# A linear-attention and mixer kernel: x tile 2 loads over GpSimd's queue, and the first query stream turns it ahead of the last weight slices

## The chip, the cores and the metric

The kernel runs on one core of a Trainium2 chip. The metric is the device time of one execution in microseconds (us). The profile shows one execution: TensorE (PE, with its weight loads as PEld), VectorE (DVE), ScalarE (ACT), GpSimd (POOL), SyncE (SP) and the DMA engines. SP, ACT and POOL each have a queue on which they issue transfers.

## The reference

Input x has 2048 tokens of width 640, all in bf16. Two branches are computed from x and mixed by a gate.

```python
g = sigmoid((x * gate_w).sum(-1, keepdims=True))
# branch A: linear attention, 32 heads of 20
q, k, v = split(x @ wqkv)                  # 640 -> 3 * 640
phi = lambda t: where(t > 0, t + 1, exp(t)) + 1e-6
pq, pk = phi(q), phi(k)
kv, z = einsum("sd,se->de", pk, v), pk.sum(over tokens)      # for each head
a = (pq @ kv) / (pq @ z + 1e-6) @ wo
# branch B: layernorm, w1, gelu, shift of tokens by quarters, w2, residual x1
#           layernorm, w3 (640 -> 1728), gelu, w4, residual
out = g * a + (1 - g) * b
```

## The kernel before

The tokens lie in 16 tiles of 128 (`NT`), the width of 640 in five slices of 128 (`KD`). A small scheduler class records every operation for its engine together with the semaphores it must wait for, and each engine then runs its own list in order. The order of the main part is chosen by a planner from modelled costs (`_Items.run`); the order of the opening, which is what matters here, is written out by hand.

The opening works like this. x tiles are loaded with tokens on the partitions (`x_tok`), and the projections need them transposed (`xT`). Tiles 0, 1 and 2 are turned by PE: `t_x(t)` transposes the five blocks of a tile against an identity `ident` (line 637 in the profile) into a bank of PSUM, and VectorE copies the bank to `xT` (line 691) in one to three pieces. Tiles 3 and later are turned by a DMA transpose on SP's queue (`x_turn`, line 281). For tile 2, `t_x` also does a small matmul of `gwr`, the gate's weights, against the identity (line 606 with the tile `xn`), which lands in the same bank; VectorE's copies of that bank come after it.

The identity is made by GpSimd (a memset of `ones_c`, then a select), in the same list in which GpSimd issues the load of the gate's weights ("gw").

The query weights `wq` come in five slices of 128 rows (wq0 to wq4), each a transfer of its own, and so do the key weights (wk0 to wk4). Transfers are issued at line 285 of the profile: x0, x1, wq2, x2, wk0, wk2, x3, wk4, x4 and then the DMA turns on SP's queue; wq0, wq1, wq3, wq4, wk1, wk3 and the last columns of wq on ACT's queue.

PE's list of the opening is: warm-up matmuls on a constant (line 904), the turn of tile 0, one more small warm-up, `q_three`, `k_two`, then one key tile, and after that a query and a key tile in turn. `q_three` is a stream (line 942): an entry (t, k) is one matmul of 512 columns that adds slice k for tile t; an entry (t, None) is the turn of tile t. Tiles 0, 1 and 2 each keep a PSUM bank until their fifth slice is in; then `phi` runs: ScalarE's exponential (line 682), VectorE's clamp (line 648) and VectorE's combining step (line 665). `k_two` is the same for the keys of tiles 0 and 1, where each entry is a pair of matmuls, of 512 and 130 columns (lines 942 and 614), in the order (0,0), (0,1), (1,0), (0,2), (1,1), (0,3), (1,2), (0,4), (1,3), (1,4).

After the opening come the gram matrix of x and the keys (lines 831 and 625), the mixer's first two products, and the large products with w3 and w4 (lines 606 and 1240).

Of the kernel before, what the change touches and what calls it, by code (L numbers as in the profile page):

```python
# [416 lines left out]
def _build(nc, A_x, A_wqkv, A_wo, B_w1, B_w2, B_w3, B_w4, gate_w, out, dbg=None, stop=None):  # L417
    sch = _Sched(nc)
# [54 lines left out]
    x_tok = pa.alloc("x_tok", [128, NT, D], BF16)  # L473
# [223 lines left out]
    x2 = A_x[0]  # L697

    def dma_in(out_ap, in_ap, key, **kw):
        return sch.dma("sp", out_ap, in_ap, key, **kw)  # L700

    def load_x(t):
        dma_in(x_tok[:, t, :], x2[128 * t:128 * (t + 1), :], "x%d" % t)

    def load_wq(k, queue):
        sch.dma(queue, wq[:, k, 0:512], A_wqkv[128 * k:128 * (k + 1), 0:512], "wq%d" % k)
# [12 lines left out]
    load_wq(1, "act")  # L719
    load_wq(2, "sp")  # L720
    load_wq(3, "act")
    load_x(2)
    load_wq(4, "act")
    load_wk(0, "sp")
    load_wk(1, "act")
# [83 lines left out]
    def phi(b, dst, after_exp=None, n=D):  # L809
        se = slot("E", 3)  # L810
        src = psf[:, 512 * b:512 * b + n]
        er = Er[:, se, 0:n]
        activation(er, src, ACTF.Exp)
        if after_exp is not None:
            after_exp()
        ts(dve, er, er, 1.0, EPS_PHI, ALU.min, ALU.add)
        return stt(dst, src, 1.0 + EPS_PHI, er, ALU.add, ALU.max)
# [108 lines left out]
    def stream(order, w, n2, done):  # L926
        bs = {}
        for t in sorted({t for t, k in order if k is not None}):
            bs[t] = pair() if n2 else bank()
            bank_hold.update((bs[t], bs[t] + 1) if n2 else (bs[t],))  # L930
        for t, k in order:
            if k is None:
                if t is None:
                    warmup(256, 0.42)
                else:
                    t_x(t)
                continue
            b = bs[t]
            l = xT[:, k, 128 * t:128 * (t + 1)]

            def fn(e, l=l, b=b, k=k):
                ins = e.matmul(ps[:, b, 0:512], l, w[:, k, 0:512], start=(k == 0), stop=(k == KD - 1))  # L942
                return ins if not n2 else mm_kept(e, ps[:, b + 1, 0:n2], l, w[:, k, 512:512 + n2], k == 0, k == KD - 1)
            pe(fn, [l, w[:, k, 0:512 + n2]], [ps[:, b, 0:512]] + ([ps[:, b + 1, 0:n2]] if n2 else []), cost=272.0 if n2 else 216.0)
            if k == KD - 1:
                bank_hold.difference_update((b, b + 1) if n2 else (b,))
                done(t, b)

    def q_three():
        order = [(0, 0), (1, None), (0, 1), (1, 0), (1, 1), (0, 2), (1, 2), (0, 3), (1, 3), (2, None), (0, 4), (1, 4),  # L950
                 (2, 0), (2, 1), (2, 2), (2, 3), (2, 4)]
        stream(order, wq, 0, lambda t, b: phi(b, pq_tok[:, t + 1, 0:512], n=512))

    def k_out(t, b):
# [10 lines left out]
    addA(("tx", 0), 0.28, lambda: t_x(0))  # L965
    addA(("warm", 1), 0.0, lambda: warmup(WARM2, 0.42))
    addA(("q", 2), 3.24, q_three)
    addA(("k", 1), 2.72, k_two)
    addA(("k", 2), 1.36, lambda: k_tile(2))
# [474 lines left out]
    order = IT.run(sch, hook)  # L1444
# [6 lines left out]
def bass_gated_mix__linear_attn_block__mixer_s_mlp__prompt_kernel(  # L1451
    nc, A_x, A_wqkv, A_wo, B_x, B_w1, B_w2, B_w3, B_w4, gate_w, out
):
    assert tuple(A_x.shape) == (1, S, D) and tuple(out.shape) == (1, S, D)
    assert tuple(A_wqkv.shape) == (D, 3 * D) and tuple(A_wo.shape) == (D, D)
    assert tuple(B_w1.shape) == (D, D) and tuple(B_w2.shape) == (D, D)
    assert tuple(B_w3.shape) == (D, F) and tuple(B_w4.shape) == (F, D) and tuple(gate_w.shape) == (D,)
    _build(nc, A_x, A_wqkv, A_wo, B_w1, B_w2, B_w3, B_w4, gate_w, out)
# [28 lines left out]
```

## Time and profile before

| | us |
|---|---|
| median of 3 runs | 259.18 (258.26 to 259.21) |
| profiled execution | 259.12 |
| its span in the profile | 257.9 |
| PE busy | 254.6 (99% of the span) |
| VectorE busy | 144.1 (56%) |
| ScalarE busy | 108.5 (42%) |
| GpSimd busy | 90.6 (35%) |

A line of the timeline gives start, duration, engine, line, operation and tiles; in square brackets is the time that the engine stood idle before it, and what released it. A list of waits has the waiting engine and line, what it waited for, the total, the number of times and the longest. A line of DMA issues ends with the median time from issue to landing. The duration of one matmul (379 ns for 512 columns) includes its way through the array; matmuls in a run start 216 ns apart.

### The profile page before, as it was taken

Reading aid. Unit: us, or ns where it says so; the run is one execution under the profiler, and the core shown is the slowest. Engines: PE = TensorE matmul, PEld = TensorE weight load, DVE = VectorE, ACT = ScalarE, POOL = GpSimd, SP = SyncE. Lnnn points to the kernel's source line nnn. Section 1 sums busy time; section 2 is a strip of 40 time slices with the busy share of each in tenths; the row PEclk is TensorE's granted clock in tenths of the full one; section 3 lists DMA queues with packets and bytes.
Section 4 is the critical chain, followed back from the end, with each engine's and each line's share of the span. In section 5 each row is a group of like instructions: output and inputs, shape, how many; then the busy total and the mean of one; then the engine's idle time right before and its main releaser. Section 6 shows DMA issues by size and latency. Waiting matters only on the chain.

```text
span 257.9 us, 3612 instructions
## 1 busy us (share of the span) xinstructions
PE 254.6 (99%) x1418; PEld 110.6 (43%) x1242; DVE 144.1 (56%) x290; ACT 108.5 (42%) x222; POOL 90.6 (35%) x146
## 2 busy tenths in 40 slices
PE   8999999999999999999999999999999999999997
PEld 4333333344454333334444444444444444444444
DVE  2697888899953995489999400689300043200033
ACT  1486676751356867665854230003520100253000
POOL 5021399967762153758907100423000011300000
DMA  6767698545843699362915520022300112200002
GB/s 209 223 170 197 145 144 223 172 86 127 108 99 78 97 335 382 85 106 51 124 40 127 127 54 20 0 82 73 51 0 0 23 20 102 102 1 3 0 20 102
DMA packets 57825, 26.48 MB, mean 103 GB/s; under 512 B 49188, under 2 KB 56397, under 8 KB 57808
## 3 DMA queue, kind: packets, MB, share of 16 engines
q1 hardware_dynamic: 54976, 21.87, 35.9%
q0 software_dynamic: 1168, 3.28, 4.9%
q10 hardware_dynamic: 1664, 1.11, 1.4%
q8 instruction: 10, 0.16, 0.3%
q14 instruction: 7, 0.06, 0.1%
HBM read 12.04 MB, written 2.62 MB: 57 GB/s over the span
## 4 chain that ended last, share of the span: by engine, by line
PE 96%; DMA 2%; SPq 0%; DVE 0%; issue 0%
PE ps L606 37%; PE ps L1240 30%; PE ps L625 14%; PE ps L831 7%; PE ps L614 4%; DMA x_tok<-in_A_x_dram 2%; PE ps L942 1%; PE ps L1286 1%; PE ps L1147 1%; SPq L285 0%; PE ps L1029 0%; PE ps L1058 0%; PE ps L637 0%; DVE x_tok L665 0%
## 5 line engine op out<-in xcount | busy, mean ns | idle before, releaser
L606 PE MATMUL ps<-xnT,w 128*128 128x512 bf16 x360 | 81.3, 379 | 0.0
L665 DVE SCALAR_TENSOR_TENSOR x_tok<-ps,stg,abx 128x512 bf16<-128x512 f32 (+2 forms) x17 | 12.2, 719 | 81.5 <-PE ps L1240 81.3
L682 ACT ACTIVATE h2T<-ps 128x512 bf16<-128x512 f32 x52 | 30.6, 598 | 59.3 <-PE ps L606 59.3
L606 PEld LDWEIGHTS ps<-xnT,w 128*128 128x128 bf16 x360 | 34.5, 98 | 41.6 <-issue 2.2
L1240 PE MATMUL ps<-w,h2T 128*128 128x512 bf16 (+2 forms) x221 | 45.4, 366 | 0.0
L648 POOL TENSOR_SCALAR xn<-x_tok,st 128x640 bf16<-128x640 bf16 x32 | 35.3, 1110 | 27.8 <-DMA xnT<-xn 27.2
L648 POOL TENSOR_SCALAR abx<-x_tok,stg 128x640 f32<-128x640 bf16 (+1 forms) x16 | 14.8, 930 | 70.0 <-DVE x_tok L665 70.0
L1240 PEld LDWEIGHTS ps<-w,h2T 128*128 128x128 bf16 x221 | 21.1, 98 | 24.1
L682 ACT ACTIVATE Er<-ps 128x512 bf16<-128x512 f32 (+1 forms) x36 | 23.0, 648 | 14.8 <-PE ps L614 10.6
L681 ACT ACTIVATE junk<-x_tok 128x640 bf16<-128x640 bf16 x32 | 23.6, 738 | 3.9 <-DVE x_tok L663 3.7
L682 ACT ACTIVATE hsT<-ps 128x512 bf16<-128x512 f32 (+1 forms) x32 | 19.0, 593 | 12.6 <-PE ps L606 12.1
L625 PE MATMUL ps<-w,hsT 128*128 128x512 bf16 x80 | 23.0, 379 | 0.0
L625 PE MATMUL ps<-wkg,xT 128*128 128x512 bf16 x70 | 20.6, 379 | 0.0
L663 DVE SCALAR_TENSOR_TENSOR x_tok<-ps,x_tok 128x640 bf16<-128x640 f32 x16 | 13.2, 822 | 10.8 <-PE ps L614 10.2
L1240 PE MATMUL ps<-M_sb,pqnT 128*128 128x512 bf16 (+2 forms) x85 | 18.6, 367 | 0.0
L831 PE MATMUL ps<-pk_tok,x_tok 128*128 128x512 bf16 x80 | 17.8, 379 | 0.0
L614 PE MATMUL ps<-wkg,xT 128*128 128x130 bf16 x80 | 17.6, 220 | 0.0
L1176 DVE TENSOR_TENSOR pq_tok<-pq_tok,dnr 128x300 bf16<-128x300 bf16 (+1 forms) x48 | 17.3, 415 | 0.6
L614 PE MATMUL ps<-w,hsT 128*128 128x128 bf16 x80 | 17.5, 219 | 0.0
L606 PE MATMUL ps<-wq,xT 128*128 128x512 bf16 x65 | 16.2, 379 | 0.0
L648 DVE TENSOR_SCALAR Er<-Er 128x512 bf16<-128x512 bf16 (+1 forms) x36 | 12.2, 340 | 6.8 <-ACT Er L682 5.9
L656 DVE TENSOR_TENSOR qprod<-qprod,pk_tok 128x640 f32<-128x640 f32 x13 | 15.1, 1165 | 0.4
(90 smaller groups left out, 252.4 us busy)
## 6 DMA issues: line engine op xcount, KB each, us to landing
w<-in_B_w_dram SPq DMA_DIRECT2D x1, 2160.0 KB, 8.1
w<-in_B_w_dram SPq DMA_DIRECT2D x1, 2080.0 KB, 13.1
out_dram<-x_tok SPq DMA_DIRECT2D x3, 640.0 KB, 3.1
w<-in_B_w_dram POOLq DMA_DIRECT2D x8, 160.0 KB, 3.4
x_tok<-in_A_x_dram SPq DMA_DIRECT2D x6, 160.0 KB, 4.1
x_tok<-in_A_x_dram SPq DMA_DIRECT2D x1, 960.0 KB, 5.5
wv<-in_A_wqkv_dram POOLq DMA_DIRECT2D x1, 800.0 KB, 5.3
x_tok<-in_A_x_dram SPq DMA_DIRECT2D x1, 640.0 KB, 5.0
```

The lines of the kernel that those rows point to most:

```text
L606: ins = e.matmul(out_ap, l, r, start=(i == 0), stop=(i == n - 1))
L614: return e.add_instruction(mybir.InstMatmult(name=nc.get_next_instruction_name(), engine=e.engine, ins=[e.lower_ap(r), ll], outs=[e.lower_ ...
L625: e.matmul(outs[0], l, r, start=st, stop=sp, skip_group_check=True)
L648: return engf(lambda e: e.tensor_scalar(out_ap, in_ap, s1, s2, op0, op1), rd, [out_ap], cost=cost)
L656: return engf(lambda e: e.tensor_tensor(out_ap, a, b_, op), [a, b_], [out_ap], cost=cost)
L663: return dve(lambda e: e.scalar_tensor_tensor(out_ap, in0, scalar, in1, op0, op1, accum_out=accum), rd, [out_ap, accum], cost=cost + 70.0)
L665: return dve(lambda e: e.scalar_tensor_tensor(out_ap, in0, scalar, in1, op0, op1), rd, [out_ap], cost=cost)
L681: return act(lambda e: e.activation(out_ap, in_ap, func, bias=bias, scale=scale, accum_out=accum), rd, wr, cost=cost)
L682: return act(lambda e: e.activation(out_ap, in_ap, func, bias=bias, scale=scale), rd, wr, cost=cost)
L831: ins = e.matmul(o, l, r, start=(t0 + q_ == 0), stop=(t0 + q_ == NT - 1))
L1176: dve(lambda e, o=o, i0=i0, i1=i1: e.tensor_tensor(o, i0, i1, ALU.mult), [i0, dnr[:, 1, sd, :]], [o], cost=cost)
L1240: ins = e.matmul(o, l, r, start=first and i == 0, stop=last and i == len(prs) - 1, skip_group_check=True)
```

## The change

x tile 2 is no longer the fourth transfer of SP's queue. It is the first transfer of GpSimd's queue, ahead of the gate's weights. In the first query stream the turn of tile 2 comes right after (1,0), and (1,1), (2,0) and (2,1) follow it; slices 2, 3 and 4 of wq then meet tiles 0, 1 and 2 one after another. The number of operations is the same on every engine; on VectorE and ScalarE their order is the same too.

```diff
     load_wq(1, "act")
     load_wq(2, "sp")
     load_wq(3, "act")
-    load_x(2)
+    sch.dma("pool", x_tok[:, 2, :], x2[256:384, :], "x2")
     load_wq(4, "act")
     load_wk(0, "sp")
     load_wk(1, "act")
...
     def q_three():
-        order = [(0, 0), (1, None), (0, 1), (1, 0), (1, 1), (0, 2), (1, 2), (0, 3), (1, 3), (2, None), (0, 4), (1, 4),
-                 (2, 0), (2, 1), (2, 2), (2, 3), (2, 4)]
+        order = [(0, 0), (1, None), (0, 1), (1, 0), (2, None), (1, 1), (2, 0), (2, 1), (0, 2), (1, 2), (2, 2),
+                 (0, 3), (1, 3), (2, 3), (0, 4), (1, 4), (2, 4)]
         stream(order, wq, 0, lambda t, b: phi(b, pq_tok[:, t + 1, 0:512], n=512))
```

## The prediction

> **What bounds the kernel now.** I read the busy table first, then the waits of TensorE (PE), then the chain of waits that ended last, and only then the first ten microseconds in detail.
>
> ```profile
> PE 254.6 (99%) x1418; PEld 110.6 (43%) x1242; DVE 144.1 (56%) x290; ACT 108.5 (42%) x222; POOL 90.6 (35%) x146
> ```
>
> PE is busy for 254.6 of 257.9 us. Asked for PE's own waits over the whole span, the trace has two:
>
> ```profile
> PE ps L904 <- PEq L1472: 0.8, 1, 0.8
> PE ps L637 <- DMA x_tok<-in_A_x_dram: 0.6, 1, 0.6
> ```
>
> The first is the start of the program. The second is the only stall on data, and it is the one that this change addresses. The chain, asked for 0 to 10 us, starts with it:
>
> ```profile
> 2.18 5.05 DMA x_tok<-in_A_x_dram
> 7.23 0.05 issue
> 7.28 0.45 PE ps L637 x5
> ...
> 7.74 1.82 PE ps L942 x8
> ```
>
> x tile 2 is issued on SP's queue at 2.18, lands at 7.23, and PE turns it at 7.28. From there PE runs without a wait to the last matmuls. So a shift of the first key matmul, now at 9.18, passes to the end one for one, and nothing else in this change can matter much. The matmul rows of the first stream say how much there is to win:
>
> ```profile
> 4.95 0.92 PE L942 MATMUL ps<-wq,xT 128*128 128x512 bf16 x3
> 5.92 0.81 PE L942 MATMUL ps<-wq,xT 128*128 128x512 bf16 x3
> 7.28 0.23 PE L637 MATMUL ps<-ident,x_tok 128*128 128x128 bf16 x1 [0.55 <-DMA x_tok<-in_A_x_dram]
> ```
>
> Matmul ends are modelled; starts in a run are 0.216 us apart. The last one before the stall starts at 6.35, so PE is really free at 6.56 and loses 0.71 us, not 0.55. Last, the DMA side, by the microsecond (busy of PE, granted clock, DMA share, GB/s):
>
> ```profile
> 2.00:3.00 1.00, 1.00 (x4) 1.00 0.97 251
> 3.00:4.00 1.00, 1.00 (x8) 1.00 0.99 333
> 4.00:5.00 1.00, 1.00 (x12) 1.00 0.96 282
> 5.00:6.00 1.00, 1.00 (x7) 1.00 0.93 281
> 6.00:7.00 1.00, 0.73 (x4) 1.00 1.05 377
> ```
>
> The 16 DMA engines are full from 2 to 9 us. Bringing one tile forward pushes others back.
>
> **The work and the floor.** From the first query matmul at 4.32 to the first key matmul at 9.18 are 4.86 us. In it lie 15 matmuls of 0.216 (3.24), ten transposes of 0.056 (0.56) and the gate's small matmul (about 0.03): 3.83 us. The first matmul and the turn of tile 1 still run partly at the slower rate (4.32 to 4.95 for what should take 0.50), so about 0.9 us is waiting and 0.1 slow rate. Were every wait to go, the gain would be 0.9 us, or 0.35%. A measurement of this kernel can tell about 0.5% (1.3 us) from no change. No case in which the change works reaches that.
>
> **x2's issue.** SP loses one issue of 0.43 us, so its later ones (wk0, wk2, x3, wk4, x4) go out 0.47 us sooner. With full DMA engines they hardly land sooner, and SP then waits 4.4 us for x3 before it turns tile 3, so this is worth nothing. GpSimd gains one issue, ahead of the gate load. The issues of its queue (size, us from issue to landing), from 1 to 1.5 us and from 38.5 to 43.1, and its timeline:
>
> ```profile
> xn<-in_gate_w_dram POOLq DMA_DIRECT2D x1, 1.2 KB, 3.4
> ...
> w<-in_B_w_dram POOLq DMA_DIRECT2D x4, 160.0 KB, 2.6
> ```
>
> ```profile
> 1.33 0.76 POOL L285 DMA_DIRECT2D xn<-in_gate_w_dram  x1 [0.83 <-DVE xn L715]
> ...
> 2.39 0.29 POOL L694 TENSOR_SCALAR_AFFINE_SELECT ident<-ones_c 128x128 bf16<-128x128 bf16 x1
> ```
>
> The other queues begin at 0.79 and x2 waits for nothing, so its issue begins near 0.8. GpSimd's issues last 0.51 to 1.01 us; it ends at 1.35 to 1.8. The gate load, which now begins at 1.33 because it waits for VectorE, moves by 0.02 to 0.5. The identity, ready at 2.68, is then ready by 3.2; PE needs it at 3.71, so this is hidden with half a microsecond to spare; past that it would cost its lateness.
>
> **When x2 lands.** Bounds: 2.6 us after issue (four loads of the same shape on GpSimd's queue, later, quieter) gives 3.4; 5.1 (x2 itself on SP now) gives 5.9. I take the gate load's 3.4, the same queue at the same place, plus 160 KB at 282 GB/s (0.57): 4.8. PE will ask for it at 5.4, so I expect no stall there. The gate load, 0.02 to 0.5 later and behind x2 on its queue, lands at 4.8 to 5.6; PE asks at 5.69.
>
> **The new order on PE.** (0,0), the turn of tile 1, (0,1) and (1,0) stand at 4.32, 4.64, 4.95 and 5.18 as now. Tile 2's turn follows at 5.40, the gate's matmul at 5.69, (1,1) at 5.72. In the present trace (2,0) starts 0.52 after the gate's matmul (7.57 to 8.09: its end, then VectorE's copy of 0.22, then the semaphore). So (2,0) starts at 6.21: a new wait of 0.27 behind (1,1), with all later matmuls queued after it. From there eleven matmuls of 0.216 (2.38) end at 8.59, where the first key matmul can start: 0.58 sooner than 9.18. That is the best case of this order.
>
> **What x2 pushes back.** x2's 160 KB now go ahead of part of x1, wq1 to wq4, at 282 GB/s 0.57 us of all engines. Bounds for x1 and wq1 (the trace has their landings at 4.34 and 4.57): none, if x2 fills gaps, as the 251 GB/s of the microsecond from 2 to 3 against 377 later allows; or the whole 0.57. The whole puts tile 1's turn at 4.95, (1,0) at 5.48 and the key matmul at 8.89. Halfway is 8.74. wq4, now at 7.5 (its issue near 2.2 plus 5.3), lands at most at 8.1. Tile 0 asks for it at 7.95 to 8.1, and the key matmul is never before wq4 plus 0.65 (three matmuls), 8.75. wk1 moves from 8.3 to at most 8.85 and is wanted 0.27 after the key start. All three agree near 8.75 to 8.8.
>
> The Trainium skill, page "DMA: Bandwidth & Descriptors", section "Issuing engines are not separate DMA queues", speaks against the change: a third issuing engine runs on the same 16 DMA engines and saves only issue time. By that rule the whole 0.57 is pushed back and the gain is 0.29; by the 2 to 3 row alone it would be 0.58. The shares of 0.93 to 1.05 side with the rule from 3 us on, so I stand between.
>
> **After the stream.** The three exponentials come close together and just before the keys. ScalarE starts at wq4 plus 0.41 as now (7.60 to 8.01), VectorE needs 0.92 per tile, so tile 1's bank is free about 2.35 after the key start. The single key tile that reuses it comes ten pairs of 0.272 (2.72) after: 0.37 to spare. Tile 3's transposed copy lands near 12.1 and its query matmul starts at 13.26, so 0.4 earlier is still covered. Memory banks, and the order on VectorE and ScalarE, are the same.
>
> **Sum.** Key start 9.18 to 8.78, gain 0.40. The profiled execution took 259.12: span 257.9 and 1.2 around it. 257.9 - 0.4 + 1.2 = 258.7. The median of the three runs is 0.06 above the profiled one: 258.8.
>
> **Rivals.**
> 1. *The wait only changes its name.* The weight slices meet three tiles each, so PE now follows wq2, wq3 and wq4, and these are what x2 delays. If wq4 lands at 8.45 rather than 8.1, the key start is 9.1 to 9.2 again: 259.1. For it: full engines, and the same bytes before the keys. Against: wq4's place in ScalarE's queue is unchanged and one tile costs 0.57 at most.
> 2. *GpSimd's queue is late* (the slower side). All of the stream now stands behind x2 and the gate load. x2 after 5.4, or the gate after 5.7, moves everything; from 0.58 beyond (x2 after 5.98) the kernel is slower than before, microsecond for microsecond. The longest landing on GpSimd's queue in the trace, 5.8, puts x2 at 6.6 and the time at 259.8; the longest of any load here, 7.2 on ScalarE's queue, puts it at 8.0 and the time at 261.2. Against: the nearest row is 3.4, and x2 is first in its queue.
> 3. *The clock comes late.* PE's matmul rate doubles at 4.64, 3.8 us after the first warm-up matmul. If x2 makes x0 late, PE pauses near 3.7. If the doubling then came one such stretch later, half of 3.8 us would be lost: 1.9, less the 0.4 gained, 260.7.
> That the change does not do what it says is excluded by the order of instructions: x2 is GpSimd's first transfer, and tile 2's turn stands after five matmuls fewer.
>
> **How the numbers follow.** Forecast 0.57 (258.5 to 259.0, with a scatter of runs of 258.26 to 259.21 before: 258.1 to 259.4). Rival 1: 0.25 (259.1). Rival 2: 0.14, about half of it past 260.5. Rival 3: 0.04, all but a little past 260.5. For eight in ten the range goes from 258.1, the forecast's best with scatter, to 259.8, the first figure of rival 2. Slower by over 0.5% is half of rival 2 and most of rival 3: 0.10. Faster by over 0.5% lies past the 0.9 us that is there, so only scatter gives it: 0.04. Within 0.5%: 0.86.
>
> **What would show it.** Right: the wait of L637 for the load of x is gone from PE's list, the turn of tile 2 starts at 5.4 to 5.7, the wait before (2,0) is near 0.3, the first key matmul starts at 8.6 to 8.9, and the span is shorter by the same amount. Rival 1: waits of L942 for the wq loads, key start near 9.2. Rival 2: L637 or the gate's matmul waits for a GpSimd load. Rival 3: transposes of 0.11 us spacing after 4.7. Wrong altogether: a key start that moves and a span that doesn't follow, which would mean a second wait behind the first that the trace of before hides.

## The result, and the profile after

The changed kernel took 260.04 us in the median of 7 runs (259.49 to 260.76), the kernel before 258.92 us beside it on the same chip (258.26 to 259.21, 7 runs). The ratio is 1.0044, with an interval of 1.0027 to 1.0061: slower by 1.1 us. The prediction was 258.8, with a range of 258.1 to 259.8. The profiled execution is the fastest of the seven (259.49, span 258.2). The changed kernel was therefore run a second time beside the experiments, and that profiled execution (260.10, span 258.8) lies at the median; the text calls it the second profile.

Of PE's own waits over the whole span, as in the first step of the prediction, the one on data:

```profile
PE ps L637 <- DMA x_tok<-in_A_x_dram: 0.6, 1, 0.6
```

The wait that the change was to remove is still there, with the same name and the same length, although PE asks 1.2 us earlier. The timeline of PE (start, duration, line, operation; in brackets the idle time before it):

```profile
4.92 0.60 PE L942 MATMUL ps<-wq,xT 128*128 128x512 bf16 x2
6.09 0.45 PE L637 MATMUL ps<-ident,x_tok 128*128 128x128 bf16 x5 [0.56 <-DMA x_tok<-in_A_x_dram]
6.66 0.18 PE L606 MATMUL ps<-ident,xn 128*128 128x5 bf16 x1
6.70 3.01 PE L942 MATMUL ps<-wq,xT 128*128 128x512 bf16 x12
9.54 0.38 PE L942 MATMUL ps<-wkg,xT 128*128 128x512 bf16 x1
```

The second matmul of the first line starts at 5.15, so PE is free at 5.37 and asks for x2 as predicted (5.4). The turn starts at 6.09, not at 5.4. Its five transposes take 0.056 each, so the gate's matmul could stand at 6.38; it stands at 6.66. The first key matmul is at 9.54, not at 8.78, and 0.36 later than in the kernel before (9.18). What holds the gate's matmul is named in the chain of waits:

```profile
1.34 0.81 POOL x_tok L285
2.15 4.46 DMA xn<-in_gate_w_dram
...
6.66 0.19 PE ps L606
...
6.87 0.24 DVE xT L691
...
7.15 2.76 PE ps L942 x12
```

The start of the chain is now GpSimd's queue. Nothing is issued on it before 1.34; then x2's issue takes 0.81, and the gate's load, 1.2 KB, is issued only at 2.15 and lands at 6.61. VectorE's copy of tile 2 needs the gate's matmul, (2,0) needs the copy, and all later matmuls of PE stand behind (2,0).

In the second profile, at the median, the same two waits are larger. PE's timeline there:

```profile
5.27 0.60 PE L942 MATMUL ps<-wq,xT 128*128 128x512 bf16 x2
6.36 0.45 PE L637 MATMUL ps<-ident,x_tok 128*128 128x128 bf16 x5 [0.49 <-DMA x_tok<-in_A_x_dram]
7.36 0.18 PE L606 MATMUL ps<-ident,xn 128*128 128x5 bf16 x1 [0.55 <-DMA xn<-in_gate_w_dram]
7.40 3.01 PE L942 MATMUL ps<-wq,xT 128*128 128x512 bf16 x12
10.25 0.38 PE L942 MATMUL ps<-wkg,xT 128*128 128x512 bf16 x1
```

Here x2 lands at 6.31 and the gate at 7.32, and the key start is 10.25: 1.07 later than before, which is the size of the whole loss.

**Everything passes to the end.** Time of the profiled execution less the start of the first key matmul: 259.12 - 9.18 = 249.94 for the kernel before, 259.49 - 9.54 = 249.95 and 260.10 - 10.25 = 249.85 for the changed one. In the profiles of all the experiments it is 249.82 to 249.95. So each kernel below can be read by one number, its key start, and that number by what lands last ahead of it.

### The profile page after: what moved, and what is told of

Its sections match the earlier page's. It is cut to its first block, busy times and chain, and to the rows that moved or that the text cites. A ratio compares the mean times of both kernels' runs of the same rounds, so it can differ in the third digit from the quotient of the medians.

```text
span 258.2 us, 3585 instructions
## 1 busy us (share of the span) xinstructions
PE 253.0 (98%) x1391; PEld 110.7 (43%) x1242; DVE 144.2 (56%) x290; ACT 108.6 (42%) x222; POOL 90.8 (35%) x147
## 4 chain that ended last, share of the span: by engine, by line
PE 90%; DVE 5%; DMA 2%; ACT 1%; issue 1%; POOL 0%; POOLq 0%
PE ps L606 34%; PE ps L1240 30%; PE ps L625 12%; PE ps L831 7%; PE ps L614 4%; PE ps L942 2%; DMA xn<-in_gate_w_dram 2%; DVE x_tok L663 1%; PE ps L1286 1%; DVE dnr L1157 1%; DVE pq_tok L1176 1%; ACT hsT L682 1%; PE ps L1147 1%; DVE qprod L656 1%; PE ps L1029 0%
## 5 line engine op out<-in xcount | busy, mean ns | idle before, releaser
L606 PE MATMUL ps<-xnT,w 128*128 128x512 bf16 x348 | 79.9, 379 | 0.6 <-issue 0.2
L682 ACT ACTIVATE hsT<-ps 128x512 bf16<-128x512 f32 (+1 forms) x32 | 19.0, 594 | 12.6 <-PE ps L606 11.1
```

The costliest lines, as they stand in the source:

```text
L606: ins = e.matmul(out_ap, l, r, start=(i == 0), stop=(i == n - 1))
L682: return act(lambda e: e.activation(out_ap, in_ap, func, bias=bias, scale=scale), rd, wr, cost=cost)
```

## The experiments

The theory after the result: the new order makes the way from x2 to the keys longer, and GpSimd's queue brings x2 and the gate too late for it. The rivals: it is the queue alone (x2 pushes the query weights back, whatever the order); it is the order alone (the queue does not matter); and, for the late landings, that GpSimd's part in the DMA traffic, or something of ScalarE's, makes them late.

The table has all kernels beside the kernel before of their own chip. "x2" and "gate" are the landings of the last part of each transfer (a transfer is spread over 16 DMA engines; PE waits for the last of the 16 parts), "key" is the start of the first key matmul, all in the profiled execution. "ACT" is ScalarE's queue, "3rd" the place on a queue.

| kernel | x2 on | gate on | order | x2 | gate | key | profiled | median | ratio (interval) |
|---|---|---|---|---|---|---|---|---|---|
| before | SP, 4th | GpSimd | old | 7.23 | 4.74 | 9.18 | 259.12 | 258.92 | 1 |
| changed | GpSimd | GpSimd, 2nd | new | 6.05 | 6.61 | 9.54 | 259.49 | 260.04 | 1.0044 (1.0027 to 1.0061) |
| changed, second time | GpSimd | GpSimd, 2nd | new | 6.31 | 7.32 | 10.25 | 260.10 | 260.04 | 1.0041 (1.0026 to 1.0056) |
| load alone | GpSimd | GpSimd, 2nd | old | 6.87 | 7.37 | 9.91 | 259.75 | 259.72 | 1.0024 (1.0007 to 1.0041) |
| order alone | SP, 4th | GpSimd | new | 6.43 | 4.72 | 9.66 | 259.49 | 260.09 | 1.0048 (1.0027 to 1.0068) |
| gate off GpSimd | GpSimd | ACT, 3rd | new | 6.00 | 4.39 | 9.35 | 259.18 | 259.21 | 1.0006 (0.9995 to 1.0017) |
| x2 on ScalarE | ACT, 3rd | GpSimd | new | 6.65 | 5.27 | 9.89 | 259.75 | 259.54 | 1.0020 (1.0001 to 1.0039) |
| nothing on GpSimd, old order | SP, 4th | ACT, 3rd | old | 6.78 | 4.50 | 9.34 | 259.17 | 259.15 | 1.0006 (0.9996 to 1.0017) |
| nothing on GpSimd, new order | ACT, 3rd | SP, 3rd | new | 6.21 | 4.50 | 9.45 | 259.27 | 259.27 | 1.0013 (1.0004 to 1.0021) |
| early exponential | SP, 4th | GpSimd, late | old | 6.90 | 10.02 | 12.81 | 262.65 | 261.91 | 1.0115 (1.0099 to 1.0131) |
| gate's matmul apart | GpSimd | GpSimd, 2nd | new | 6.97 | 7.48 | 10.20 | 260.15 | 259.41 | 1.0019 (1.0006 to 1.0031) |
| gate apart, turn later | GpSimd | GpSimd, 2nd | another | 6.12 | 6.96 | 9.43 | 259.25 | 259.26 | 1.0012 (0.9998 to 1.0025) |
| load alone, gate apart | GpSimd | GpSimd, 2nd | old | 6.06 | 6.58 | 9.16 | 258.99 | 259.37 | 1.0021 (1.0007 to 1.0034) |
| x2 third on SP | SP, 3rd | GpSimd | new | 6.41 | 4.97 | 9.87 | 259.70 | 259.48 | 1.0020 (1.0009 to 1.0030) |

A profiled execution is one draw: the same x2 transfer, fourth on SP's queue, landed at 7.23, 6.43, 6.78 and 6.90 in four kernels. Size is therefore read from the ratios, mechanism from the profiles.

### The load alone

On the kernel before, with its order:

```diff
-    load_x(2)
+    sch.dma("pool", x_tok[:, 2, :], x2[256:384, :], "x2")
```

> Only the load is moved: x2 is GpSimd's first transfer, the stream keeps its old order. Theory A (the changed kernel loses because x2 and the gate load come late over GpSimd's queue and the new order puts the whole stream behind them): x2 lands near 6.05 and the gate near 6.6 as in the changed kernel, but the old order asks for them only at 6.56, so the stall on x2 falls from 0.7 to 0.1 us, the first key matmul starts at 9.0 to 9.1 and the time is 0.1 to 0.2 us below before (258.7 to 258.8). Theory C (x2's early bytes push the weight slices back): wq4 lands at 8.0 or later, seven matmuls follow it, the first key matmul starts at 9.5 or later, 0.3 to 0.5 us above before (259.3).

The ratio is 1.0024, and the wait has another name in PE's list:

```profile
PE ps L942 <- DMA wq<-in_A_wqkv_dram: 1.2, 2, 1.1
```

This is the prediction's first rival, in a kernel other than the one it was meant for: x2 goes ahead of the query weights, and these are what PE asks for first in the old order. wq2 lands at 6.78 and wq3 at 7.54; in the kernel before they landed at 5.34 and 5.60, and PE did not wait for them. It is their last parts that come late: the middle part of wq2 landed at 4.65, sooner than the 4.90 of the kernel before, and the last 2.1 us behind it. That x2's bytes hold those last parts back is argued and not shown; with the same transfers wq2 landed at 5.88 and 4.90 in the two profiles of the changed kernel. The turn of tile 2 stands behind (1,3), so x2 at 6.87 is early enough, and the gate at 7.37 too.

### The order alone

The new `order` of `q_three`, with x2 fourth on SP's queue.

> Only the order is changed: tile 2 is turned right after (1,0), but x2 stays the fourth transfer of SP's queue. Theories A and B (the order itself costs) agree: PE stands from 5.4 until x2 lands near 7.2, (2,0) starts 0.8 us after that, eleven matmuls follow, the first key matmul starts near 10.4 to 10.5 and the time is 1.2 to 1.4 us above before (260.2). It gives the price per us of lateness of x2 in this order. Theory C: the same.

The ratio is 1.0048, as much as that of the whole change:

```profile
6.47 0.45 PE L637 MATMUL ps<-ident,x_tok 128*128 128x128 bf16 x5 [0.94 <-DMA x_tok<-in_A_x_dram]
```

From x2's landing at 6.43 to the key start are 3.23 us. With the same transfer in the old order it was 7.23 to 9.18, that is 1.95. The 1.28 between them are five more matmuls behind the turn (twelve, not seven: 5 x 0.216 = 1.08) and some 0.2 of the wait before (2,0), which (1,1) alone covers now. The same 3.23 to 3.24 stand in the kernels with x2 on ScalarE, with nothing on GpSimd in the new order and with the gate's matmul apart. So the new order needs x2 by 9.18 - 3.23 = 5.95, and no profile has it before 6.00. The 9.18 is that of one execution (259.12). The median of the kernel before, 258.92, answers to a key start of 258.92 - 249.95 = 8.97, and by that the new order needs x2 by 5.74 already.

Load alone (0.6 us) and order alone (1.2) do not add up to the change (1.1). The likely reason, not tested by itself: with the load the weights come later, but the new order asks for them later too.

### The gate's load off GpSimd's queue

On the changed kernel; the gate's load becomes the third transfer of ScalarE's queue:

```diff
     load_wq(1, "act")
+    sch.dma("act", xn[0:KD, 1, 0:128], gate_w.rearrange("(k p) -> k p", p=128), "gw")
...
-    sch.dma("pool", xn[0:KD, 1, 0:128], gate_w.rearrange("(k p) -> k p", p=128), "gw")
```

> The changed kernel, but the gate's weights load as the third transfer of ScalarE's queue, so they no longer stand behind x2 on GpSimd's. Theory A: the gate lands before 5.2, the wait of its matmul (0.27 us in the profiled execution) goes, x2 still lands near 6.05, the first key matmul starts near 9.25 and the time is about 0.3 us below the changed kernel (259.6 to 259.8). Theory B: no gain, since the order is kept (260.0). Theory C: no gain or 0.1 us.

The ratio falls from 1.0041 to 1.0006: 0.9 of the 1.1 us are gone, and the kernel can no longer be told from the kernel before.

```profile
6.04 0.45 PE L637 MATMUL ps<-ident,x_tok 128*128 128x128 bf16 x5 [0.49 <-DMA x_tok<-in_A_x_dram]
6.33 0.17 PE L606 MATMUL ps<-ident,xn 128*128 128x5 bf16 x1
```

The gate's matmul follows the last transpose at once (6.33, where the second profile of the changed kernel has 1.0 from the turn to it). The wait for x2 stays. The key start is x2 + 3.35: by x2 it would be 9.23, and the rest is wq4, which lands at 8.64 behind the gate's load on its queue. The 0.9 need not be the gate's landing alone: here GpSimd issues one load less, and x2's first data moved at 3.67, where the two profiles of the changed kernel have 4.04 and 4.16.

### x2 on ScalarE's queue

On the changed kernel; GpSimd has the gate's load alone again:

```diff
     load_wq(1, "act")
+    sch.dma("act", x_tok[:, 2, :], x2[256:384, :], "x2")
...
-    sch.dma("pool", x_tok[:, 2, :], x2[256:384, :], "x2")
```

> The changed kernel's order, with x2 as the third transfer of ScalarE's queue (ahead of wq3) instead of GpSimd's; the gate load stays GpSimd's only early transfer. Theory A: x2 lands at 5.2 to 5.6, the gate at 4.7, the order finds its data in time, the first key matmul starts at 8.6 to 8.9 and the time is 0.3 to 0.6 us below before (258.3 to 258.6). Theory B: the order costs whatever the queue, so it stays 0.5 us or more above before (259.4 or more). Theory C: wq3 and wq4 are pushed back by a whole tile, the first key matmul starts near 9.2 or later and the time is that of before or 0.3 us above (259.0 to 259.2).

```profile
6.70 0.45 PE L637 MATMUL ps<-ident,x_tok 128*128 128x128 bf16 x5 [1.02 <-DMA x_tok<-in_A_x_dram]
```

x2, issued at 1.72, lands at 6.65: 4.9 us from issue to landing, where GpSimd's queue took 4.7 and 5.0. The ratio is 1.0020 (259.54, in the range of theory B). The middle one of its 16 parts lands at 5.29, the last 1.36 us behind it. So a slow GpSimd queue is not what makes x2 late; a wait of half a microsecond to one for x2 stays whichever queue it is on.

### The changed kernel again

> The changed kernel once more, beside the kernels of this call. All theories: 259.9 to 260.3, 0.8 to 1.2 us above before. Its profiled execution was its fastest (259.49); theory A says that an execution of the median time has the gate's last part, behind x2, landing near 7.2 instead of 6.61, and the first key matmul near 10.1 instead of 9.54; were the key start not later than 9.6 in an execution near 260.0, the loss would lie elsewhere.

The result repeats: 260.04 again, 1.0041. Its timeline is shown with the result above. PE waits in it for both loads, and its landings say what each costs when the execution is a median one. The sum closes: x2 at 6.31 + 3.23 = 9.54 is 0.36 more than before; the gate adds 10.25 - 9.54 = 0.71. Together 1.07.

### Nothing on GpSimd's queue, in both orders

If GpSimd's traffic were what makes the last parts late, they should come in time without it. In the old order:

```diff
     load_wq(1, "act")
+    sch.dma("act", xn[0:KD, 1, 0:128], gate_w.rearrange("(k p) -> k p", p=128), "gw")
...
-    sch.dma("pool", xn[0:KD, 1, 0:128], gate_w.rearrange("(k p) -> k p", p=128), "gw")
```

> The kernel before, but the gate's weights load as the third transfer of ScalarE's queue: GpSimd's queue carries nothing in the opening. In every profile so far the DMA rate falls from 330 to 380 GB/s to 150 to 250 between 4 and 5.5 us, and some of the 16 DMA engines fall a microsecond behind. Theory D1 (GpSimd's first transfers make that dip): the dip is gone, x2 lands at 6.2 to 6.4 instead of 7.23, PE does not stand, the first key matmul starts at 8.5 to 8.6 and the time is 0.4 to 0.6 us below before. Theory D2 (ScalarE's table load at 4.14 makes it) and D3 (neither): the dip stays, x2 lands near 7, the time is that of before within 0.2 us.

Here x2's landing decides nothing. The gate's load stands ahead of wq3 on ScalarE's queue, wq3 lands at 6.96 (5.60 in the kernel before), and PE waits for it before it asks for x2:

```profile
PE ps L942 <- DMA wq<-in_A_wqkv_dram: 0.9, 1, 0.9
```

So this kernel answers the question on the rate, but its time says nothing of what an earlier x2 would be worth.

In the new order the gate's load is third on SP's queue and x2 third on ScalarE's:

```diff
     load_x(1)
+    sch.dma("sp", xn[0:KD, 1, 0:128], gate_w.rearrange("(k p) -> k p", p=128), "gw")
     load_wq(1, "act")
+    sch.dma("act", x_tok[:, 2, :], x2[256:384, :], "x2")
...
-    sch.dma("pool", x_tok[:, 2, :], x2[256:384, :], "x2")
...
-    sch.dma("pool", xn[0:KD, 1, 0:128], gate_w.rearrange("(k p) -> k p", p=128), "gw")
```

> The changed kernel's order with x2 as the third transfer of ScalarE's queue and the gate's weights as the third of SP's: GpSimd's queue carries nothing in the opening. D1: no dip, x2 lands by 5.5, the first key matmul starts at 8.6 to 8.9, 0.3 to 0.6 us below before (258.5). D2 and D3: x2's last part lands near 6.5 as with GpSimd's gate load (6.65), the key start is 9.6 to 9.9 and the time 0.4 to 0.8 us above before.

The DMA rows by the half microsecond (length, busy of PE, granted clock, DMA share, GB/s), first of the old order, then of the new:

```profile
4.50:5.00 0.50, 0.50 (x8) 1.00 0.83 200
5.00:5.50 0.50, 0.50 (x4) 1.00 1.10 336
```

```profile
4.50:5.00 0.50, 0.50 (x7) 1.00 0.63 115
5.00:5.50 0.50, 0.45 (x2) 1.00 0.76 222
```

In the half microsecond before these rows it is 321 and 322. Without any load on GpSimd's queue the rate still falls to 200 and 115 GB/s just before 5 us, and x2's last part still comes at 6.78 and 6.21, with its middle one at 5.73 and 4.72. Loads on GpSimd's queue do not make the dip. The ratios, 1.0006 and 1.0013, show no gain.

### An early exponential on ScalarE

The other suspect for the dip was the load of ScalarE's table for the exponential. To move it, a small exponential was put behind the issue of wq4, on the kernel before:

```diff
-    gwr = xn[:, 1, 0:128]
+    gwr = xn[:, 1, 0:128]; gwd = junk[:, 0, 0:2]
...
-    load_wq(4, "act")
+    load_wq(4, "act"); act(lambda e: e.activation(gwd, gwr[:, 0:2], ACTF.Exp), [gwr[:, 0:2]], [gwd])
```

> The kernel before, with an exponential of two elements on ScalarE after its fourth transfer, whose result is not used; it brings the table load from 4.14 to about 2.7. D2 (the table load makes the dip of the DMA rate): the dip moves to 3 to 4 us, x2 lands nearer 6.4 and the time falls by up to 0.5 us. D1 and D3: the dip stays at 4 to 5.5 us and the time is that of before within 0.2 us; wk1, wk3 and the last columns of wq are issued 1.3 us later, which their slack covers or which costs up to 0.3.

The edit had a side effect that spoils its time. The exponential reads the tile into which the gate's load writes, so that load, and with it all of GpSimd's list, had to wait:

```profile
4.49 0.76 POOL L285 DMA_DIRECT2D xn<-in_gate_w_dram  x1 [3.99 <-ACT junk L723]
```

The identity came near 5.8, and PE, after a wait of 2.1 us, began the turn of tile 0 at 5.99 instead of 3.71. That is 2.3 of the 3.6 us by which the key start is late (12.81); the other 1.3 go with PE's rate: its matmuls start 0.43 apart, twice the usual 0.216, until 11.1. One reading survives this, from the DMA rows of this kernel (columns as above):

```profile
4.00:4.50 0.50, 0.00 (x0) 1.00 0.76 250
4.50:5.00 0.50, 0.00 (x0) 1.00 0.96 259
5.00:5.50 0.50, 0.00 (x0) 1.00 0.95 294
```

The table load had moved to 2.69 to 3.97, PE did nothing at all in these stretches, and the rate was still low, 250 to 294. That speaks against the table load and against PE's work as the cause; it does not exclude that the dip has moved, since other transfers moved too.

### The gate's matmul apart from tile 2

On the changed kernel, with the same transfers: the gate's matmul and the copy of its result leave tile 2's bank and go to one of their own, just before (0,4). An entry (None, None) of the order now calls `gate_col`.

```diff
     def t_x(t):
...
-            if t == 2:
-                mm_group(ps[:, b, 448:448 + KD], [(gwr, ident[:, 0:KD])])
...
-            if t == 2:
-                copy(dve, wkg[:, :, D + 1:D + 2], ps[:, b, 448:448 + KD].rearrange("p (k o) -> p k o", o=1))
...
+    def gate_col():
+        b = bank()
+        mm_group(ps[:, b, 448:448 + KD], [(gwr, ident[:, 0:KD])])
+        copy(dve, wkg[:, :, D + 1:D + 2], ps[:, b, 448:448 + KD].rearrange("p (k o) -> p k o", o=1))
...
-                    warmup(256, 0.42)
+                    gate_col()
...
-                 (0, 3), (1, 3), (2, 3), (0, 4), (1, 4), (2, 4)]
+                 (0, 3), (1, 3), (2, 3), (None, None), (0, 4), (1, 4), (2, 4)]
```

> The changed kernel with the same transfers on the same queues; only the gate's small matmul and its copy have a PSUM bank of their own and stand just before (0,4), so tile 2's copies no longer wait for the gate's weights. Theory A, now in two terms (the gate's load behind x2, and x2's own last part): PE waits for x2 until 6.05 to 6.3 as in the two profiles of the changed kernel, (2,0) follows 0.8 us later, the first key matmul starts at 9.2 to 9.5, and the time is 0.5 to 0.8 us below the changed kernel (259.2 to 259.5). Theory C (the weight slices that x2 pushed back take the place of any wait removed): 259.8 to 260.0.

The ratio is 1.0019, where the changed kernel has 1.0041: 0.6 us back with the same loads on the same queues. That is the price of the gate's landing, measured a second way, though less sharply: the two intervals overlap between 1.0026 and 1.0031. The profiled execution is the slowest of the twelve, and PE's only wait on data in it is for x2:

```profile
7.01 0.45 PE L637 MATMUL ps<-ident,x_tok 128*128 128x128 bf16 x5 [0.67 <-DMA x_tok<-in_A_x_dram]
```

Its gate lands at 7.48, and nothing waits for it.

### The gate apart, and the turn later

The same, but tile 2 is turned after (1,2), and (0,3) and (1,3) stand between its turn and (2,0):

```diff
+        order = [(0, 0), (1, None), (0, 1), (1, 0), (1, 1), (0, 2), (1, 2), (2, None), (0, 3), (1, 3), (2, 0),
+                 (2, 1), (2, 2), (2, 3), (None, None), (0, 4), (1, 4), (2, 4)]
```

> As the kernel with the gate apart, but tile 2 is turned after (1,1), (0,2) and (1,2), and (0,3) and (1,3) stand between its turn and (2,0), so that they cover x2's last part and VectorE's copies. Theory A: PE asks for x2 near 6.15, waits at most 0.2, the first key matmul starts at 8.7 to 9.0, bound by wq3 and wq4, and the time is 0.1 to 0.4 us below before (258.5 to 258.9), the fastest version. Theory C: wq2 and wq3 land 0.5 to 1.3 us later than in the kernel before (5.34 and 5.60), PE waits for them under line 942, the key start is 9.3 to 9.6 and the time 0.2 to 0.5 us above before (259.2 to 259.5).

The ratio is 1.0012 with an interval that holds 1. The list of waits of PE's matmuls has no wait on data, and yet the key start is 9.43. Two things make it so, and the rows of PE and of its weight loads (PEld) show both:

```profile
5.27 2.01 PE L942 MATMUL ps<-wq,xT 128*128 128x512 bf16 x5
7.12 0.44 PE L637 MATMUL ps<-ident,x_tok 128*128 128x128 bf16 x5
```

```profile
6.55 0.14 PEld L942 LDWEIGHTS ps<-wq,xT 128*128 128x128 bf16 x2 [0.59 <-DMA wq<-in_A_wqkv_dram]
```

The first four of these matmuls start about 0.43 apart, and the usual 0.216 comes only near 6.9; in the profile of before and in the first one of the changed kernel it comes at 4.57 to 4.64. But the fourth of them, (0,2), could not start sooner at any rate: its weight load waits for wq2, which lands at 6.51 (5.34 in the kernel before), and the matmul starts at 6.56. The slow matmuls before it filled the time in which PE would have stood, so no wait shows under PE. After 6.56 the slow rate costs one matmul 0.34 instead of 0.216, some 0.13 us. The rest is the late wq2, as theory C had it, and the time is theory C's (259.2 to 259.5).

### The load alone, with the gate apart

The kernel before, x2 first on GpSimd's queue, and the gate's matmul apart, just before (0,4).

> The old order with x2 as GpSimd's first transfer (as in the run of the load alone, 259.72) and the gate's matmul apart, just before (0,4). Theory A (the gate behind x2 made the load alone slow): the 0.7 us go, time 258.7 to 259.0. Theory C (wq2 and wq3, pushed back by x2's early bytes, made it slow): it stays at 259.5 to 259.8, and the waits of PE are under line 942 for the weights.

```profile
PE ps L942 <- DMA wq<-in_A_wqkv_dram: 0.4, 1, 0.4
```

The ratio is 1.0021, nearly that of the load alone (1.0024); the time, 259.37, lies between the two theories and nearer to C. In the old order nobody waits for the gate, so to set it apart buys nothing, and what the load costs shows as a wait for the query weights (here for wq2, at 6.12). This profile is the kernel's fastest execution: wq3 landed at 6.74 (7.54 in the load alone), and the key start 9.16 equals that of before.

### x2 third on SP's queue

On the changed kernel; x2 ahead of wq2 on SP, the gate's load alone on GpSimd:

```diff
     load_x(1)
     load_wq(1, "act")
+    load_x(2)
     load_wq(2, "sp")
...
-    sch.dma("pool", x_tok[:, 2, :], x2[256:384, :], "x2")
```

> The changed kernel's order with x2 as the third transfer of SP's queue, ahead of wq2 (which becomes the fourth), and the gate's load alone on GpSimd's queue as in the kernel before. In the profiles so far the third transfer of SP has landed with its last part at 5.3 to 5.9 (once 6.8), the gate alone on GpSimd's queue at 4.7 to 5.3. Theory A (in this order the key start is x2's last part plus 3.2): key start 8.6 to 9.1, unless wq2, now in x2's old place (6.4 to 7.2), binds with its own plus 2.0: 8.5 to 9.2. Time 0 to 0.4 us below before. Theory C': whichever transfer stands there, its last part comes at 6.0 to 6.5 while the engines lag, key start 9.3 to 9.6, 0.2 to 0.5 us above before.

x2 lands at 6.41 with its middle part at 5.16, and the ratio is 1.0020; this is near theory C', whose key start of 9.3 to 9.6 is passed. The expectation's row for theory A was too narrow: the 128 KB load of wq2, where it is third on SP's queue, landed its last part at 4.9 to 6.8 in the profiles before this one, not at 5.3 to 5.9. By x2 the key start would be 9.64; wq2, pushed to 7.87, makes it 9.87. The lag of the last parts is there on the third queue as well. No kernel of the table is faster than the kernel before.

## Why the prediction was wrong

**The steps that failed: when x2 and the gate's load land.** The prediction's sum for x2 was an issue near 0.8 and a landing 3.4 + 0.57 later, 4.8. Three terms of it were too small.

- "Its issue begins near 0.8". It began at 1.34, with nothing to wait for. The trace of before had shown the gate's load beginning at 1.33 and named VectorE as the releaser; the prediction believed the name. The memset that it meant had ended at 0.99 (0.88 and 0.11), a third of a microsecond before. The first issue on GpSimd's queue stands at 1.33 to 1.34 in every kernel that loads over it, save the one with the early exponential, while with no load there GpSimd's first memset runs at 0.79. So the 0.54 belongs to the first issue of that queue. It moves x2 and the gate alike.
- "3.4 plus 0.57". From the issue's start to the landing it took 4.7 in the profile, 5.0 in the second one, 0.7 to 1.0 more than the 4.0 taken. The row of 3.4 was that of a 1.2 KB load, issued alone; the tile's own row, 5.1 on SP's queue and listed as the upper bound, was the nearer one. The middle part of x2 landed at 5.19 and 5.17, only 0.4 after the 4.8; the last, for which PE waits, at 6.05 and 6.31.
- "The gate load lands at 4.8 to 5.6". It landed at 6.61 and 7.32. This is the larger part of the loss: its issue went from 1.33 to 2.15, since x2's issue comes first and takes 0.81, and its way took 4.5 and 5.2 instead of 3.4. The prediction had the load only 0.02 to 0.5 later and priced the new wait on it at nothing. Out of the way, it is worth up to 0.9 us (gate off GpSimd) or 0.6 (gate's matmul apart); the closing sum of the second profile says 0.71.

For the first of these: VectorE's memset in the kernel before, x2's issue in the changed kernel, and GpSimd's first memset of the program's own list with nothing on its queue (old order):

```profile
0.88 0.11 DVE L715 MEMSET xn<- 128x64 uint32 x1 [0.88 <-PEq L1472]
```

```profile
1.34 0.82 POOL L285 DMA_DIRECT2D x_tok<-in_A_x_dram  x1 [0.83 <-POOLq L1472]
```

```profile
0.79 0.20 POOL L685 MEMSET ones_c<- 128x128 bf16 x1 [0.29 <-POOLq L1472]
```

For the others: the DMA issues of the two profiles (KB, us from issue to landing), first the changed kernel's, then the second time's:

```profile
x_tok<-in_A_x_dram POOLq DMA_DIRECT2D x1, 160.0 KB, 4.7
xn<-in_gate_w_dram POOLq DMA_DIRECT2D x1, 1.2 KB, 4.5
```

```profile
x_tok<-in_A_x_dram POOLq DMA_DIRECT2D x1, 160.0 KB, 5.0
xn<-in_gate_w_dram POOLq DMA_DIRECT2D x1, 1.2 KB, 5.2
```

**Rival 2 is what happened,** with its break-even: it said that past 5.98 for x2 the kernel is slower than before, microsecond for microsecond, and the runs put that point at 5.95. Its argument "x2 is first in its queue" did not help, and its chance of 0.14 was too low because the forecast rested on one row of another size. Only the name of the rival is too narrow: x2 on ScalarE's queue or third on SP's lands no sooner.

**What held.** The shift of the key start passes to the end one for one (249.82 to 249.95 in every profile). PE asks for x2 at 5.37 in the first profile, predicted 5.40. The distance from the gate's matmul to (2,0) is 0.50, predicted 0.52. The identity is ready at 3.29 and wanted at 3.68, predicted 3.2 and 3.71: hidden. SP's later loads did land sooner (x3 at 8.65 and 8.96, 9.53 before), but no wait of PE is on them. wq4 landed at 7.51 and 7.89 and did not bind. The rule of the Trainium skill that the prediction weighed (page "DMA: Bandwidth & Descriptors", section "Issuing engines are not separate DMA queues") fits the runs, in which no queue brings x2 in clearly sooner than another: x2's last part came at 6.00 to 6.97 from GpSimd's queue, at 6.21 and 6.65 from ScalarE's, at 6.41 to 7.23 from SP's.

**Rival 1** (the wait turns to wq) appeared where the old order was kept and in the order with the later turn: PE waited for wq2 or wq3 in the load alone, with the gate apart or not, in the old order with nothing on GpSimd's queue, and, under its weight loads, with the turn later. In the new order it added 0.1 us with the gate off GpSimd (wq4) and 0.2 with x2 third on SP's queue (wq2). In the changed kernel itself it did not appear.

**Rival 3** (the clock comes late) had the right sign and not the right reason. Near-equal openings differ in when the matmul spacing halves: near 5.2 in the second profile of the changed kernel, after 5.7 with the gate apart, near 6.9 with the turn later, and 4.57 to 4.64 in the two profiles compared first. In the three late ones x0 had landed at 3.64 to 3.66 (3.67 before) and PE did not pause, so x2 did not bring it about in the way the rival says; and waits on loads cover nearly all of it. Only in the early exponential did PE pause (from 3.9 to 6.0) and pay for the late rate, 1.3 us.

**What stays open.** Why the rate falls, to between 115 and 266 GB/s in its lowest half microsecond from 4 to 6 us, in every profile, and why the last of x2's 16 parts comes 0.4 to 1.9 us behind the middle one. Loads on GpSimd's queue are excluded; the table load and PE's work are made unlikely. No experiment changed the number of bytes asked for ahead of 4 us, which would be the next one.

## What to carry to other kernels

A load is wanted by the time at which its last part lands, and the row to price it by is the same size in the same full stretch, not a small one that had its queue to itself. An order that brings work forward also moves all the rest behind the load that this work needs: compute the landing at which it breaks even (here 5.95 at the latest) and ask whether any row of the trace is that early. And count who else sits behind on the queue: here a 1.2 KB load behind the tile cost more than the tile. And where PE shows no wait, look at its weight loads too: they can wait for a slice while slow matmuls fill the time.

## What was not expected of the hardware

- The first transfer issue on GpSimd's queue begins at 1.33 to 1.34 even with nothing to wait for, 0.55 us after those of the other queues. x2's first data then moved 1.5 to 2.1 us after its issue had ended (at 4.04 in the changed kernel, whose issue ended at 2.15); x0's on SP's queue moved 0.6 us after (1.82 and 1.19).
- In the full opening x2's last part came 0.4 to 1.9 us behind its middle one, 1.1 in the median of the 14 profiles: 0.9 to 1.9 on GpSimd's queue, 1.4 and 1.5 on ScalarE's, 0.4 to 1.2 on SP's.
- PE's rate doubled at times from about 3.7 us (nothing on GpSimd's queue, old order) to about 6.9 (the turn later) in kernels whose PE instructions were the same up to 3.6, while the granted clock in the rows read 1.00 throughout; the spacing of the matmuls shows it, that column does not. The Trainium skill (page "TensorE: Matmul & The Clock Gate", part 1, "What's actually happening") says that the clock follows a window that runs free of the kernel's start, and that the transition varies by 500 ns either way for this. A moving transition is what these runs show; its spread here is 3.2 us, more than the page has, and here the measurement counts.
